# The last stage of a three-part kernel: out-weight conversion at the end of each block, plain products between the Strassen products, a branch moved earlier, and pools moved to other addresses

## The chip, the cores and the metric

The program runs on one core of a Trainium2 chip. The metric is the device time of one execution in microseconds (us); the median of several executions is compared. Five engines matter: PE (matrix products into PSUM banks), DVE and ACT (element work, both read PSUM), POOL (element work without PSUM) and SP (issues DMA). Each engine takes its own instructions strictly in the order in which they are written, and waits where an operand is not ready.

## What is computed

```python
a = x @ w_a            # x: 1536 x 512, from the two stages ahead (attention, a mixture of 8 experts)
b = x @ w_b            # w_a, w_b: 512 x 1536
out = (a * b) @ w_out  # w_out: 1536 x 512
```

The weights of this third part come in as 64-bit floats. The change is in this part, and at the end of the expert part, where it is prepared.

## The kernel before

Every float32 operand is split into a high part of a shorter format and a low remainder (`...h`, `...l`), and a product is three PE instructions: high by high, low by high, high by low. One such instruction streams 512 columns of its moving operand past 128 columns of weights that it loads first; the text calls it "a product".

The third part works on 12 blocks `f` of 128 columns of `w_a` and `w_b`, and on three row groups `c` of 512 tokens. Its token matrix has been put together by the experts in `y_dram`; row group 0 is `yT`, row groups 1 and 2 are loaded with `xload` into `XF` and split by `ysp`. Weights go through four steps per half block: `cload` (DMA issued by SP), `conv1` (two ACT instructions), `conv2` (three DVE instructions and one POOL add, L902), `conv3` (ACT cast of the high part, L913, and POOL subtraction for the low part, L914). The output weights `w_out` take the same steps; their halves are called `wo` and stand in `MW[12]` to `MW[17]`.

Blocks 0 and 1 are computed plainly: `first` (row group 0, 48 products), `plain(1, ..)` and `plain(2, ..)` (48 products each). For blocks 2 to 11 there is `seven(f)`. It computes row groups 0 and 1 with a Strassen scheme of seven half-size products on sums `S1` to `S4` of the tokens (made by `ssum` and `ysp`) and on sums of the weights (`tsum` on DVE, `tsplit` on ACT and POOL). The scheme takes 42 products on three banks `pa`, `pb`, `pc`. Its fifth product (`S3`) and its last (`A22`) both add into bank `pb`, and between them DVE reads the bank (L1292), so `A22` has to wait for that read. Row group 2 is computed plainly by `ab2` (24 products on `Y2`, "P2" in the title; P3, P5 and P7 are the Strassen products on `S3`, `S4` and the second half of `yT`); its result is multiplied on DVE (L1260) and split by `gate` (ACT L1186, DVE L1187).

After each odd block the two blocks' results meet the output weights: `both` puts 12 tiles in a list, and `fill(n)` takes n of them. `out_tile` is six products into one of three banks `o`, and one element instruction that adds the bank to the accumulator in `XF`. A pair of blocks has 6 tiles behind its odd block and 6 inside the next even one.

Between the experts and `seven` stands a branch (`tc.If`, L1067) that is not taken on these inputs. Whatever the branch might write counts as written by it: an instruction behind it that reads or overwrites such a tile waits until the writing engine has passed the branch, and an engine passes only when it has finished what it had before it. Ahead of the branch, DVE has the sums of the tokens (L1042) and `conv2` for the first output weights.

Tiles lie in pools that are stacked from the left (low addresses) or from the right end of SBUF. Before, the weights' pool `wA` starts at byte 20,000 of a partition, the pool `bg` (token accumulators, some expert weights, `S4`) at 52,768, the token sums and `Y2` at 85,536 to 134,688, the gate results `gh`, `gl` at 138,784 to 165,408, the pool `wM` (weights of block 0 and the output weights) at 176,096, and `yT` at 212,960.

Of the kernel before, what the change touches and what calls it, by code (L numbers as in the profile page):

```python
# [19 lines left out]
ALU = mybir.AluOpType  # L20
# [26 lines left out]
def moe_block_kernel(ctx, tc, qd, kd, vd, kt, vn, nv, wg, wg2, we, wm, out):  # L47
# [40 lines left out]

    wA = ctx.enter_context(tc.tile_pool(name="wA", bufs=4))
    bgp = ctx.enter_context(tc.tile_pool(name="bg", bufs=8, reuse_waits="tile"))  # L90

# [662 lines left out]

    def xload(c, g):
        if (c, g) not in XF:
            XF[c, g] = big("acc")[:, :].rearrange("p (k n) -> p k n", k=2)
        nc.sync.dma_start(XF[c, g], y_dram[2 * g:2 * g + 2, :, c * 512:(c + 1) * 512].rearrange("d p n -> p d n"))

# [164 lines left out]
    def ysplit(st, g, eng, yT):  # L924
# [15 lines left out]
        (6, 4): [(cload, nc.scalar)], (6, 8): [(cload, nc.scalar)],  # L940
        (7, 8): [(conv1, (1, 0))], (7, 9): [(conv2, (1, 0))], (7, 10): [(conv1, (1, 1))], (7, 11): [(conv2, (1, 1))],
        (7, 12): [(cload, nc.sync)], (7, 13): [(cload, nc.sync)], (7, 14): [(cload, nc.sync)],
    }
    for k, n in enumerate(CAPS):
        X = XT.pop(k)
        Hm = htiles(epp, n)
        nxt = tiles(CAPS[k + 1]) if k < NE - 1 else []
        gs = []

        def W(c):  # L950
            return EW[k, c]

        def tick(i):
            if k == 0 and i == 0:
                COL.extend(regs(range(7), [ACT], NTOK, "counts of tokens before an expert, or all tokens"))
                COL.extend(regs([7], [SP], NTOK, "counts of tokens before an expert, or all tokens"))
            if k == 1 and i == 0:
                rare.append(nc.values_load(ctl_i[0:1, 16:17], min_val=0, max_val=1, skip_runtime_bounds_check_because="a flag"))
            if k == 0 and i == 1:
                r_base()  # L960
                rt.append(r_token(ps, "h", 6, sc, i128, i96[:, 0:NT], tokid))
            if k < 2 and i % 4 == 2:
                next(rt[0], None)
            if k == 1 and i == 14:
                rsc.close()
                yp, pools["V"], pools["M"] = (
                    ctx.enter_context(tc.tile_pool(name=n_, bufs=1, side="right", reuse_waits="tile")) for n_ in ("yp", "cv", "wM"))
# [24 lines left out]
        for f in range(8):  # L992
            up(W, f, X, n, Hm, epp)
            if f == 2 and yq:
                yq.pop(0)()
            tick(f)
        for d in range(4):
            yq.append(down(W, d, Hm, n, COL[k], epp, bg=lambda h, d=d: tick(8 + 2 * d + h), q=nc.scalar if nxt else nc.sync))
            if d:
                yq.pop(0)()  # L1000
# [12 lines left out]

    def first():
        for (f, s_), pt in N0.items():
            mul(pt, wab(f, s_), yT, True)

    yq.pop(0)()
    for h in range(2):
        conv3((1, h))  # L1020
# [20 lines left out]
    def ssum(o, a, b, op):  # L1041
        V.tensor_tensor(o, a, b, op)  # L1042

    def sums():
        ssum(XF[1, 1], XF[1, 0], XF[1, 1], ALU.add)
        ssum(XF[1, 0], XF[0, 0], XF[1, 0], ALU.subtract)
        ssum(XF[0, 0], XF[1, 1], XF[0, 0], ALU.subtract)
        ssum(XF[0, 1], XF[0, 1], XF[0, 0], ALU.subtract)

    def c12(*js):  # L1050
        for j in js:
            conv1(j)
        conv2(*js)
        for _ in js:
            cload(nc.sync)

    for g in range(2):
        xload(2, g)
    ysp(XF[1, 0], S4, V)
    ysp(XF[1, 1], A22, V)  # L1060
    for h, l in (Y2, S2, S1, S3):
        A.copy(h[:, 0, 0:2], ident[:, 0:2])
        V.tensor_copy(l[:, 0, 0:2], ident[:, 0:2])
    sums()
    c12((12, 0), (12, 1))

    with tc.If(rare[0] == 1):  # L1067
        with ExitStack() as ls:
# [75 lines left out]
            lqs.close()  # L1144
            for c in (1, 0, 2):
                for g in range(2):
                    xload(c, g)
            for g in range(2):
                ysp(XF[0, g], [y[:, 2 * g:2 * g + 2] for y in yT], V)
            ysp(XF[1, 0], S4, V)  # L1150
            ysp(XF[1, 1], A22, V)
            sums()
            first()

# [33 lines left out]

    def evict(c, f, pp, h1=(), h2=()):

        a = tmp("a")
        A.copy(a, pp[0])
        run_all(h1)
        V.tensor_tensor(pp[1], a, pp[1], ALU.mult)
        low = gate(c, f, pp[1])
        run_all(h2)
        low()

    def plain(c, f, tags, h1=(), h2=()):

        pp = [t_ if not isinstance(t_, str) else bank(t_, {"ab": 2, "o": 3}.get(t_, 1)) for t_ in tags]
        for s_, pt in enumerate(pp):
# [3 lines left out]
            else:  # L1206
                mul(pt, wab(f, s_), Y2, True)
        evict(c, f, pp, h1, h2)

    def run_all(fs):  # L1210
        for f_, *x in fs:
            f_(*x)

    outs, items = [], []

    def out_tile(p, c, t_):
        po = bank("o", 3)
        for i, f in enumerate((2 * p, 2 * p + 1)):
# [4 lines left out]
            T.matmul(po, gl, wh, start=False, stop=(i == 1))  # L1223
        m, at = 4 * c + t_, XF[c, t_ // 2][:, t_ % 2]
        if p == 0:
            (A.copy if t_ % 2 else V.tensor_copy)(at, po)
        else:
            V.tensor_tensor(at, po, at, ALU.add)  # L1228
# [8 lines left out]
    def fill(n):  # L1237
        for _ in range(n):
            if items:
                out_tile(*items.pop(0))  # L1240

    def seven(f):

# [5 lines left out]
        nxt = [(f + 2, 0), (f + 2, 1)] if f < 10 else []  # L1249
        nxt += [WO[f + 1]] if f + 1 in WO else []  # L1250
        a = tmp("a")
# [10 lines left out]

        def side():
            if jobs:
                tsum(f + 1)
                tsplit(f + 1)
                conv2(*wo)
                for j in jobs + wo:
                    conv3(j)
                for _ in nxt:  # L1270
                    cload(nc.sync)

# [21 lines left out]
        V.tensor_tensor(u2, pc, u2, ALU.add)  # L1294
# [7 lines left out]
        low[1]()  # L1302
        for j in nxt:
            conv1(j)
# [8 lines left out]
    def both(p):  # L1313
        items.extend((p, c, t_) for c in (2, 0, 1) for t_ in range(4))
    evict(0, 0, (N0[0, 0], N0[0, 1]), (), [(conv3, (12, 0))])
    evict(0, 1, (N0[1, 0], N0[1, 1]), (), [(conv3, (12, 1))])
    pse.close()
    ps2 = ctx.enter_context(tc.tile_pool(name="ps2", bufs=1, space=PSUM, reuse_waits="tile"))
    pab = [bank("ab", 2) for _ in range(2)]
    for g in range(2):  # L1320
        ysp(XF[2, g], [y[:, 2 * g:2 * g + 2] for y in Y2], V)
    c12((2, 0), (2, 1))
    plain(1, 0, ("o", "pc"), (), [(tsum, 2), (conv3, (2, 0)), (conv3, (2, 1))])
    plain(1, 1, ("pa", "pb"), (), [(tsplit, 2), (ysp, XF[0, 0], S2, V)])
    plain(2, 0, pab, [(ysp, XF[1, 1], S1, V)], [(ysp, XF[0, 1], S4, V)])
    plain(2, 1, ("o", "pc"), [(ysp, XF[1, 0], S3, V)])
    c12((13, 0))
    for j in ((3, 0), (3, 1), (13, 1)):
        conv1(j)
    both(0)  # L1330
    fill(6)
    conv3((13, 0))
    for f in range(2, 12):
# [46 lines left out]
```

## Time and profile before

| | us |
|---|---|
| median of 3 runs | 629.22 (628.03 to 629.35) |
| the profiled execution, time | 632.77 |
| the profiled execution, span of its instructions | 631.1 |
| PE busy in the span | 575.5 (91%) |
| DVE, ACT, POOL busy | 419.8, 307.0, 246.9 |

The span runs from the first to the last profiled instruction. The third part begins at 299.5 us of the span. Busy time counts a waiting product not at all, and a product at a lower clock as longer.

### The profile page before, as it was taken

What the parts mean: (1) busy time and instruction counts of PE and PEld (TensorE: products, weight loads), DVE (VectorE), ACT (ScalarE), POOL (GpSimd) and SP (SyncE); (2) the same over time, 40 slices, a digit from 0 to 9 for tenths busy, and PEclk for the clock granted to TensorE, in tenths of its full rate; (3) what the DMA queues carried; (4) which work ended last, traced back from release to release, by engine and by line L of the source; (5) the groups of instructions that cost most, each with busy time, mean ns of one, the idle gap of its engine ahead of it and who ended that gap; (6) DMA issues with size and microseconds to landing.
All of it is one profiled execution on the core that took longest, in us unless ns stands there. A gap on an engine that the chain in (4) does not pass through costs nothing. (4 is left out here: it accounts for less than half of the span.)

```text
span 631.1 us, 9995 instructions
## 1 busy us (share of the span) xinstructions
PE 575.5 (91%) x3395; PEld 488.9 (77%) x3395; DVE 419.8 (67%) x988; ACT 307.0 (49%) x685; POOL 246.9 (39%) x227
## 2 busy tenths in 40 slices
PE   6998995799999999999894999899899899989994
PEld 4776774699999988999683788688688688778873
DVE  6878786686546868768766455576666576567462
ACT  5776881465566677765365434314405224331210
POOL 3000641544444645454342353334414614414224
PEclk9999997699999999999998899899899999979998
DMA  8477474467757798776530021111220302210013
GB/s 289 136 214 263 142 214 169 148 205 258 216 181 255 225 320 244 245 251 203 180 115 18 34 100 66 34 66 55 80 68 33 101 27 75 66 33 1 1 57 143
DMA packets 38656, 87.24 MB, mean 138 GB/s; under 512 B 5920, under 2 KB 16416, under 8 KB 38592
## 3 DMA queue, kind: packets, MB, share of 16 engines
q1 hardware_dynamic: 31680, 73.55, 35.7%
q10 hardware_dynamic: 4752, 6.00, 3.0%
q0 software_dynamic: 2160, 6.91, 3.0%
q8 instruction: 31, 0.51, 0.3%
q14 instruction: 33, 0.27, 0.1%
HBM read 73.25 MB, written 13.20 MB: 137 GB/s over the span
## 5 line engine op out<-in xcount | busy, mean ns | idle before, releaser
L117 POOL TENSOR_TENSOR wl<-st,wh 128x512 fp32r<-128x512 f32 x54 | 69.8, 1312 | 88.6 <-ACT wh L112 81.8
L902 POOL TENSOR_TENSOR tx<-tx,st 128x512 int32<-128x512 int32 x36 | 51.5, 1444 | 115.4 <-ACT p L1274 54.2
L112 ACT CAST wh<-st 128x1024 fp32r<-128x1024 f32 x64 | 67.3, 1054 | 31.1 <-DMA st<-we 30.5
L117 DVE TENSOR_TENSOR wl<-st,wh 128x1024 fp32r<-128x1024 f32 x37 | 53.3, 1442 | 29.0 <-ACT wh L112 28.7
L727 PE MATMUL ps_h<-x,wl 128*128 128x256 f32 (+5 forms) x256 | 69.8, 272 | 0.0
L727 PE MATMUL ps_y<-h,wl 128*128 128x256 f32 (+5 forms) x256 | 68.6, 268 | 0.0
L1221 PE MATMUL ps_o<-wh,gh 128*128 128x512 f32 x144 | 60.2, 418 | 7.0 <-ACT gh L1186 6.2
L1228 DVE TENSOR_TENSOR acc<-ps_o,acc 128x512 f32<-128x512 f32 x60 | 40.9, 690 | 34.0 <-PE ps_o L1223 31.8
L1223 PE MATMUL ps_o<-wh,gl 128*128 128x512 f32 x144 | 59.4, 412 | 1.9 <-DVE gl L1187 1.9
L1222 PE MATMUL ps_o<-wl,gh 128*128 128x512 f32 x144 | 59.9, 416 | 0.0
L523 ACT ACTIVATE pe<-pe,mx 128x256 f32<-128x256 f32 (+1 forms) x96 | 45.9, 480 | 22.4 <-DVE mx L519 22.4
L914 POOL TENSOR_TENSOR wl<-tx,wh 128x512 fp32r<-128x512 f32 x36 | 47.3, 1336 | 19.6 <-ACT wh L913 9.4
L723 PE MATMUL ps_y<-h,wh 128*128 128x448 f32 (+3 forms) x160 | 50.1, 372 | 2.8 <-DVE h L741 2.8
L727 PEld LDWEIGHTS ps_h<-x,wl 128*128 128x128 f32 x256 | 49.9, 195 | 0.0
L727 PEld LDWEIGHTS ps_y<-h,wl 128*128 128x128 f32 x256 | 48.5, 189 | 0.0
L1175 POOL TENSOR_TENSOR wl<-tt,wh 128x512 fp32r<-128x512 f32 x20 | 28.4, 1441 | 51.0 <-ACT wh L1173 51.0
L723 PE MATMUL ps_h<-x,wh 128*128 128x448 f32 (+3 forms) x160 | 48.2, 366 | 0.0
L1221 PEld LDWEIGHTS ps_o<-wh,gh 128*128 128x128 f32 x144 | 28.8, 200 | 15.5 <-ACT gh L1186 7.2
L519 DVE CUSTOM_DVE_ANT_0 pe<-ps_s,bias 128x256 f32<-128x256 f32 (+1 forms) x96 | 32.8, 398 | 8.2 <-PE ps_s L513 7.3
L1223 PEld LDWEIGHTS ps_o<-wh,gl 128*128 128x128 f32 x144 | 28.9, 201 | 9.9 <-DVE gl L1187 2.7
L913 ACT CAST wh<-tx 128x512 fp32r<-128x512 f32 x36 | 21.3, 619 | 28.5 <-POOL tx L902 28.5
L1222 PEld LDWEIGHTS ps_o<-wl,gh 128*128 128x128 f32 x144 | 28.9, 201 | 7.0
(317 smaller groups left out, 1526.6 us busy)
## 6 DMA issues: line engine op xcount, KB each, us to landing
st<-we SPq DMA_DIRECT2D x63, 512.0 KB, 4.7
st<-wm SPq DMA_DIRECT2D x32, 512.0 KB, 3.5
vc<-vd SPq DMA_DIRECT2D x16, 352.0 KB, 3.9
k<-kd SPq DMA_DIRECT2D x7, 464.0 KB, 7.0
y_dram<-zero SPq DMA_DIRECT2D x12, 256.0 KB, 6.5
x_dram<-x SPq DMA_DIRECT2D x6, 512.0 KB, 4.7
acc<-y_dram SPq DMA_DIRECT2D x6, 512.0 KB, 5.9
q<-qd SPq DMA_DIRECT2D x7, 384.0 KB, 5.9
```

Of the source, the lines that this page charges most:

```text
L112: A.copy(wh, st)
L117: eng.tensor_tensor(wl[:, r], st[:, r], wh[:, r].bitcast(F32), ALU.subtract)
L519: V.tensor_tensor_reduce(out=pe[:, t_, j, 0:n], in0=ps[:, j, t_, 0:n], in1=bias[2 * p + j][:, b0:b0 + n], op0=ALU.add, op1=ALU.min, scale= ...
L523: A.activation(pe[:, t_, j, 0:n], pe[:, t_, j, 0:n], AF.Exp, bias=mx[:, t_, j:j + 1], scale=-1.0, accum_out=sm[:, t_, j:j + 1])
L723: T.matmul(pt[:, 0:2 * n].rearrange("p (s n) -> p s n", s=2), a, M[:, k], start=(k == 0), stop=False)
L727: T.matmul(pt[:, 0:n], b, M[:, k, 0], start=False, stop=(k == last))
L902: lambda t=txi, l=l: G.tensor_tensor(t, t, l, ALU.add)))
L914: G.tensor_tensor(wl_, tx, wh.bitcast(F32), ALU.subtract)
L1221: T.matmul(po, gh, wh, start=(i == 0), stop=False)
L1222: T.matmul(po, gh, wl, start=False, stop=False)
L1223: T.matmul(po, gl, wh, start=False, stop=(i == 1))
L1228: V.tensor_tensor(at, po, at, ALU.add)
```

## The change

1. **Order inside `seven`.** `conv2` and the load of the output weights move from the middle of a block to its end (`rest`), and their `conv3` goes to the next block, behind the `conv3` of the block weights (`late`). In odd blocks `ab2(1)` and its split stand ahead of every `conv3`. The six products `A12` into bank `pa` move from ahead of `ab2(1)` to between `S3` and `S4`.
2. **Start of the third part.** The branch stands behind 24 of the 48 products of `first`; the other 24, the loads of row group 2, the token sums and `conv2` of the first output weights come behind it, interleaved with the plain products. Eight output tiles (before: six) run ahead of `seven(2)`; the first 12 tiles' copies are all on ACT, in another order of row groups. `conv3` of block 1 and `conv1` of the first output weights go into the last expert; one load moves into the expert before it.
3. **Places.** `wA` and `bg` are stacked from the right. Now the token sums and `Y2` lie at 20,000 to 69,152, `gh`, `gl` at 75,296 to 99,872, `wM` at 110,560, `yT` at 126,944, `bg` at 163,808 and `wA` at 196,576.

```diff
-    wA = ctx.enter_context(tc.tile_pool(name="wA", bufs=4))
-    bgp = ctx.enter_context(tc.tile_pool(name="bg", bufs=8, reuse_waits="tile"))
+    wA = ctx.enter_context(tc.tile_pool(name="wA", bufs=4, side="right"))
+    bgp = ctx.enter_context(tc.tile_pool(name="bg", bufs=8, side="right", reuse_waits="tile"))
...
-        (7, 12): [(cload, nc.sync)], (7, 13): [(cload, nc.sync)], (7, 14): [(cload, nc.sync)],
+        (6, 14): [(cload, nc.sync)], (7, 12): [(cload, nc.sync)],
+        (7, 13): [(conv3, (1, 0)), (conv1, (12, 0))], (7, 15): [(conv3, (1, 1)), (conv1, (12, 1))],
...
-    first()
+    first(0)
...
-    ysp(XF[1, 0], S4, V)
-    ysp(XF[1, 1], A22, V)
...
-    sums()
-    c12((12, 0), (12, 1))
 
     with tc.If(rare[0] == 1):
...
-        def side():
-            if jobs:
-                tsum(f + 1)
-                tsplit(f + 1)
-                conv2(*wo)
-                for j in jobs + wo:
-                    conv3(j)
-                for _ in nxt:
-                    cload(nc.sync)
+        def rest():
+            for j in wo:
+                c2(j)
+                late.append((conv3, j))
+            for j in nxt:
+                conv1(j)
...
             fill(4)
-        side()
-        mul(pa, wab(f, 0, 2, 4), A12, False, True, True)
+        if jobs:
+            tsum(f + 1)
+            tsplit(f + 1)
         if f % 2:
             ab2(1)
             low[2]()
-        else:
+        for j in jobs:
+            conv3(j)
+        while late:
+            f_, j = late.pop(0)
+            f_(j)
+        for j in wo:
+            conv1(j)
+        for _ in nxt:
+            cload(nc.sync)
+        if f % 2 == 0:
             fill(2)
         mul(pb, T3, S3, False, True, True)
         V.tensor_tensor(v, pb, v, ALU.add)
+        mul(pa, wab(f, 0, 2, 4), A12, False, True, True)
         mul(pc, wab(f, 1, 2, 4), S4, False, True, True)
...
         if f % 2:
             both(f // 2)
-            fill(6 if f < 11 else 12)
+            fill(3)
+            rest()
+            fill(3 if f < 11 else 9)
         else:
             ab2(0)
+            rest()
             ab2(1)
             low[2]()
...
+    for g in range(2):
+        xload(2, g)
+    first(1)
+    c2((12, 0), (12, 1))
+    e = [evict(0, f, (N0[f, 0], N0[f, 1])) for f in range(2)]
+    ysp(XF[1, 0], S4, V)
...
+    both(0, (0, 1, 2))
+    e[1]()
+    ysp(XF[0, 0], S2, V)
+    fill(2)
+    ssum(XF[0, 1], XF[0, 1], XF[0, 0], ALU.subtract)
+    conv3((2, 0))
+    fill(1)
+    ysp(XF[0, 1], S4, V)
+    conv3((2, 1))
+    fill(1)
```

ACT in an odd block (`seven(5)`), from the copy of the first Strassen product to the split of `ab2`'s result, before:

```order
L1258 COPY a<-ps_ab 128x512
L1173 CAST wh<-tt 128x1024
L913 CAST wh<-tx 128x512 x3
L1186 CAST gh<-ps_ab 128x512
L1186 CAST gh<-ps_pa 128x512
```

and in the changed kernel, the same place (its lines are numbered anew):

```order
L1237 COPY a<-ps_ab 128x512
L1146 CAST wh<-tt 128x1024
L1159 CAST gh<-ps_ab 128x512
L913 CAST wh<-tx 128x512 x3
L885 ACTIVATE tx<-st_6823 128x512
L887 ACTIVATE st_6823<-st_6823 128x512
L1159 CAST gh<-ps_pa 128x512
```

The cast `gh<-ps_ab` has moved ahead of the three `conv3` casts, and a `conv1` pair stands where none was.

POOL in the same block, before: two adds of the block weights, the two low halves of the weight sums, the add of the output weights and three low parts.

```order
L902 TENSOR_TENSOR tx<-tx,st_6794 128x512
L902 TENSOR_TENSOR tx<-tx,st_6796 128x512
L1175 TENSOR_TENSOR wl<-tt,wh 128x512 x2
L902 TENSOR_TENSOR tx<-tx,st_6798 128x512
L914 TENSOR_TENSOR wl<-tx,wh 128x512 x3
```

and in the changed kernel:

```order
L902 TENSOR_TENSOR tx<-tx,st_6748 128x512
L902 TENSOR_TENSOR tx<-tx,st_6750 128x512
L1148 TENSOR_TENSOR wl<-tt,wh 128x512 x2
L914 TENSOR_TENSOR wl<-tx,wh 128x512 x3
L902 TENSOR_TENSOR tx<-tx,st_6823 128x512
```

The add of the output weights now follows the three low parts, the last of which belongs to the output weights that were added one block earlier.

DVE ahead of the branch, from the last expert results on, before:

```order
L749 TENSOR_TENSOR yt<-ps_y,yt 128x176 x3
L1039 TENSOR_TENSOR S4l<-acc,S4h 128x1024
L1039 TENSOR_TENSOR A22l<-acc,A22h 128x1024
L1063 CAST Y2l<-ident 128x2
L1063 CAST S2l<-ident 128x2
L1063 CAST S1l<-ident 128x2
L1063 CAST S3l<-ident 128x2
L1042 TENSOR_TENSOR acc<-acc 128x1024 x4
L897 TENSOR_SCALAR tx<-tx 128x512 x2
L899 TENSOR_SCALAR tx<-tx 128x512 x2
L900 SCALAR_TENSOR_TENSOR tx<-st_5267,tx 128x512
L900 SCALAR_TENSOR_TENSOR tx<-st_5277,tx 128x512
```

and in the changed kernel:

```order
L749 TENSOR_TENSOR yt<-ps_y,yt 128x176
L897 TENSOR_SCALAR tx<-tx 128x512
L899 TENSOR_SCALAR tx<-tx 128x512
L900 SCALAR_TENSOR_TENSOR tx<-st_4969,tx 128x512
L749 TENSOR_TENSOR yt<-ps_y,yt 128x176 x3
L1043 COMPARE_AND_BRANCH
```

Between the last expert result and the branch nothing is left on DVE; the splits, the sums and `conv2` stand behind it.

## Rows read from the trace of the kernel before

**Rows 1.** Windows, third part: us, busy (instructions) of PE, PEld, DVE, ACT, POOL; clock.

```profile
299.50:357.87 58.37, 47.47 (x183) 36.59 (x182) 38.04 (x56) 29.28 (x50) 18.41 (x13) 0.88 0.30 95
357.87:622.30 264.43, 251.99 (x1057) 202.97 (x1055) 161.57 (x284) 81.90 (x139) 106.08 (x83) 0.97 0.17 57
```

**Rows 2.** Waits of PE, third part: line, released by, total us, times, longest.

```profile
PE ps_pb L1007 <- DVE v L1292: 12.4, 4, 3.1
PE ps_o L1221 <- ACT gh L1186: 6.2, 2, 4.7
```

**Rows 3.** The chain that ended last, inside `seven(5)`: start us, us, step.

```profile
446.44 1.25 POOL tx L902
447.72 0.62 ACT wh L913
448.33 0.49 ACT gh L1186
448.85 0.69 DVE gl L1187
449.54 0.61 DVE v L1292
450.20 0.50 PE ps_pb L1007
```

**Rows 4.** Timeline of PE in `seven(4)` and `seven(5)`: start us, us, instruction.

```profile
413.86 0.39 PE L1221 MATMUL ps_o<-wh,gh 128*128 128x512 f32 x1
...
419.46 0.39 PE L1007 MATMUL ps_pa<-yTh,wh 128*128 128x512 f32 x1
...
427.76 0.39 PE L1007 MATMUL ps_ab<-Y2h,wh 128*128 128x512 f32 x1
...
433.20 0.39 PE L1007 MATMUL ps_pa<-yTh,wh 128*128 128x512 f32 x1
...
434.60 0.39 PE L1007 MATMUL ps_pb<-S2h,wh 128*128 128x512 f32 x1
...
451.41 0.63 PE L1008 MATMUL ps_pb<-A22l,wh 128*128 128x512 f32 x1
451.84 0.63 PE L1009 MATMUL ps_pb<-A22h,wl 128*128 128x512 f32 x1
```

**Rows 5.** Timelines of DVE, POOL and ACT around the branch; brackets: idle before, releaser.

```profile
305.57 4.99 DVE L1042 TENSOR_TENSOR acc<-acc 128x1024 f32<-128x1024 f32 x4
312.63 2.88 POOL L902 TENSOR_TENSOR tx<-tx,st 128x512 int32<-128x512 int32 x2 [9.48 <-DVE tx L900]
315.60 0.58 ACT L1192 COPY a<-ps_n 128x512 f32<-128x512 f32 x1 [10.00 <-POOLq L1067]
```

**Rows 6.** Timelines of POOL in `seven(4)` and `seven(5)`, and of ACT in `seven(5)`.

```profile
422.98 2.78 POOL L1175 TENSOR_TENSOR wl<-tt,wh 128x512 fp32r<-128x512 f32 x2 [7.38 <-ACT wh L1173]
...
438.02 2.90 POOL L902 TENSOR_TENSOR tx<-tx,st 128x512 int32<-128x512 int32 x2 [7.24 <-issue]
443.68 2.76 POOL L1175 TENSOR_TENSOR wl<-tt,wh 128x512 fp32r<-128x512 f32 x2 [2.75 <-ACT wh L1173]
447.64 3.74 POOL L914 TENSOR_TENSOR wl<-tx,wh 128x512 fp32r<-128x512 f32 x3
442.55 1.05 ACT L1173 CAST wh<-tt 128x1024 fp32r<-128x1024 f32 x1 [1.65 <-DVE tt L1168]
```

**Rows 7.** Timelines of POOL and DVE just ahead of the branch.

```profile
300.60 2.55 POOL L914 TENSOR_TENSOR wl<-tx,wh 128x512 fp32r<-128x512 f32 x2 [2.33 <-ACT wh L913]
302.08 2.15 DVE L1039 TENSOR_TENSOR S4l<-acc,S4h 128x1024 fp32r<-128x1024 f32 x1 [1.70 <-ACT S4h L1037]
304.15 1.21 DVE L1039 TENSOR_TENSOR A22l<-acc,A22h 128x1024 fp32r<-128x1024 f32 x1
```

**Rows 8.** Timeline of PE in `first`, weights in `wM`: start us, us, instruction.

```profile
303.19 0.39 PE L1008 MATMUL ps_n<-yTl,wh 128*128 128x512 f32 x1
...
304.55 0.39 PE L1008 MATMUL ps_n<-yTl,wh 128*128 128x512 f32 x1
```

More of the change, by code (lines that the diff above doesn't have):

```diff
@@ L940, in moe_block_kernel @@
         (6, 4): [(cload, nc.scalar)], (6, 8): [(cload, nc.scalar)],
-        (7, 8): [(conv1, (1, 0))], (7, 9): [(conv2, (1, 0))], (7, 10): [(conv1, (1, 1))], (7, 11): [(conv2, (1, 1))],
-        (7, 12): [(cload, nc.sync)], (7, 13): [(cload, nc.sync)], (7, 14): [(cload, nc.sync)],
+        (7, 8): [(conv1, (1, 0))], (7, 9): [(conv2, (1, 0))], (7, 10): [(conv1, (1, 1)), (cload, nc.sync)], (7, 11): [(conv2, (1, 1))],
+        (6, 14): [(cload, nc.sync)], (7, 12): [(cload, nc.sync)],
+        (7, 13): [(conv3, (1, 0)), (conv1, (12, 0))], (7, 15): [(conv3, (1, 1)), (conv1, (12, 1))],
     }
@@ L955, in tick @@
                 COL.extend(regs(range(7), [ACT], NTOK, "counts of tokens before an expert, or all tokens"))
-                COL.extend(regs([7], [SP], NTOK, "counts of tokens before an expert, or all tokens"))
+                COL.extend(regs([7], [SP, ACT], NTOK, "counts of tokens before an expert, or all tokens"))
             if k == 1 and i == 0:
@@ L965, in tick @@
                 rsc.close()
-                yp, pools["V"], pools["M"] = (
-                    ctx.enter_context(tc.tile_pool(name=n_, bufs=1, side="right", reuse_waits="tile")) for n_ in ("yp", "cv", "wM"))
+                pools["V"], yp, pools["M"] = (
+                    ctx.enter_context(tc.tile_pool(name=n_, bufs=1, side="right", reuse_waits="tile")) for n_ in ("cv", "yp", "wM"))
                 yT.extend(yp.tile([P, 4, 512], F32R, name=n_) for n_ in ("yTh", "yTl"))
@@ L997, in moe_block_kernel @@
         for d in range(4):
-            yq.append(down(W, d, Hm, n, COL[k], epp, bg=lambda h, d=d: tick(8 + 2 * d + h), q=nc.scalar if nxt else nc.sync))
+            yq.append(down(W, d, Hm, n, COL[k], epp, bg=lambda h, d=d: tick(8 + 2 * d + h), q=nc.scalar if nxt or d == 3 else nc.sync))
             if d:
@@ L1012, in wab, with first @@
         return [w[:, :].rearrange("p (s k n) -> p s k n", s=2, k=4)[:, s_, k0:k1] for w in MW[f]]
-    def first():
-        for (f, s_), pt in N0.items():
-            mul(pt, wab(f, s_), yT, True)
+    def first(f):
+        for s_ in range(2):
+            mul(N0[f, s_], wab(f, s_), yT, True)
     yq.pop(0)()
-    for h in range(2):
-        conv3((1, h))
     N0 = {(f, s_): ps.tile([P, 512], F32, tag="h", bufs=6, name="ps_n") for f in range(2) for s_ in range(2)}
-    first()
+    first(0)
     ep.close()
@@ L1042, in ssum @@
         V.tensor_tensor(o, a, b, op)
[L1044 to L1054, printed above, removed]
-            cload(nc.sync)
-    for g in range(2):
-        xload(2, g)
-    ysp(XF[1, 0], S4, V)
-    ysp(XF[1, 1], A22, V)
-    for h, l in (Y2, S2, S1, S3):
-        A.copy(h[:, 0, 0:2], ident[:, 0:2])
-        V.tensor_copy(l[:, 0, 0:2], ident[:, 0:2])
-    sums()
-    c12((12, 0), (12, 1))
     with tc.If(rare[0] == 1):
@@ L1144, in moe_block_kernel @@
             lqs.close()
-            for c in (1, 0, 2):
+            for c in (1, 0):
                 for g in range(2):
-                    xload(c, g)
+                    xload(c, g, nc.scalar)
             for g in range(2):
                 ysp(XF[0, g], [y[:, 2 * g:2 * g + 2] for y in yT], V)
[L1150 to L1153, printed above, removed]
+            first(0)
     m2 = ctx.enter_context(tc.tile_pool(name="m2", bufs=1, side="left", reuse_waits="tile"))
@@ L1187, in gate, with evict, first_, second @@
         return lambda: V.tensor_tensor(gl, a, gh[:, :].bitcast(F32), ALU.subtract)
-    def evict(c, f, pp, h1=(), h2=()):
+    def evict(c, f, pp):
         a = tmp("a")
[L1192 to L1199, printed above, removed]
+        def first_():
+            A.copy(a, pp[0])
+            V.tensor_tensor(pp[1], a, pp[1], ALU.mult)
+        def second():
+            gate(c, f, pp[1])()
+        return first_, second
+    def plain(c, f, tags):
         pp = [t_ if not isinstance(t_, str) else bank(t_, {"ab": 2, "o": 3}.get(t_, 1)) for t_ in tags]
@@ L1207, in plain @@
                 mul(pt, wab(f, s_), Y2, True)
[L1208 to L1212, printed above, removed]
+        return pp
     outs, items = [], []
@@ L1223, in out_tile @@
             T.matmul(po, gl, wh, start=False, stop=(i == 1))
-        m, at = 4 * c + t_, XF[c, t_ // 2][:, t_ % 2]
+        m, at = 4 * c + t_, XF[(c + 2) % 3, t_ // 2][:, t_ % 2]
         if p == 0:
-            (A.copy if t_ % 2 else V.tensor_copy)(at, po)
+            A.copy(at, po)
         else:
@@ L1240, in fill, with c2 @@
                 out_tile(*items.pop(0))
+    late = []
+    def c2(*js):
+        conv2(*js)
+        for _ in js:
+            cload(nc.sync)
     def seven(f):
@@ L1249, in seven @@
         nxt = [(f + 2, 0), (f + 2, 1)] if f < 10 else []
-        nxt += [WO[f + 1]] if f + 1 in WO else []
         a = tmp("a")
@@ L1288, in seven @@
             low[2]()
-        else:
+        for j in jobs:
[6 more added lines that the diff above has]
+        for _ in nxt:
+            cload(nc.sync)
+        if f % 2 == 0:
             fill(2)
@@ L1302, in seven, with both, ev @@
         low[1]()
-        for j in nxt:
-            conv1(j)
         if f % 2:
             both(f // 2)
-            fill(6 if f < 11 else 12)
+            fill(3)
+            rest()
+            fill(3 if f < 11 else 9)
         else:
             ab2(0)
+            rest()
             ab2(1)
             low[2]()
[L1313 to L1316, printed above, removed]
+    def both(p, order=(2, 0, 1)):
+        items.extend((p, c, t_) for c in order for t_ in range(4))
+    def ev(c, f, pp):
+        for f_ in evict(c, f, pp):
+            f_()
+    for g in range(2):
[4 more added lines that the diff above has]
+    ysp(XF[1, 0], S4, V)
+    e[0][0]()
+    e[0][1]()
+    ysp(XF[1, 1], A22, V)
+    conv1((2, 0))
+    ev(0, 1, (N0[1, 0], N0[1, 1]))
     pse.close()
@@ L1319, in moe_block_kernel @@
     pab = [bank("ab", 2) for _ in range(2)]
+    p10, p11 = plain(1, 0, ("o", "pc")), plain(1, 1, ("pa", "pb"))
+    for h in range(2):
+        conv3((12, h))
     for g in range(2):
         ysp(XF[2, g], [y[:, 2 * g:2 * g + 2] for y in Y2], V)
[L1322 to L1332, printed above, removed]
+    conv1((2, 1))
+    ssum(XF[1, 1], XF[1, 0], XF[1, 1], ALU.add)
+    ev(1, 0, p10)
+    c2((2, 0), (2, 1))
+    ev(1, 1, p11)
+    p20, p21 = plain(2, 0, pab), plain(2, 1, ("o", "pc"))
+    ev(2, 0, p20)
+    tsum(2)
+    tsplit(2)
+    conv1((13, 0))
+    ssum(XF[1, 0], XF[0, 0], XF[1, 0], ALU.subtract)
+    e = evict(2, 1, p21)
+    e[0]()
+    ssum(XF[0, 0], XF[1, 1], XF[0, 0], ALU.subtract)
+    both(0, (0, 1, 2))
[8 more added lines that the diff above has]
+    fill(1)
+    ysp(XF[1, 1], S1, V)
+    fill(1)
+    conv1((3, 0))
+    fill(1)
+    ysp(XF[1, 0], S3, V)
+    conv1((3, 1))
+    fill(2)
+    c2((13, 0))
+    late.append((conv3, (13, 0)))
     for f in range(2, 12):
```

5 lines of the change are left out of this document (2 added, 3 removed).

## The prediction

> **What bounds the kernel now.** I read the windows of the third part first. PE is busy in 252.0 of the 264.4 us from 357.87 on, and in 47.5 of the 58.4 us before that, at granted clocks of 0.97 and 0.88 [rows 1]; DVE comes next with 161.6 and 38.0 us. So PE is the bound, and what can be gained is the time in which it waits or runs at the lower of its two levels (1.2 instead of 2.4 GHz). To see how much that is, I work out what the same products cost without either, from the starts of products in the timeline: 24 of row group 2 begin within 433.20 - 427.76 = 5.44 us, that is 0.2267 us each, and 24 of output tiles within 419.46 - 413.86 = 5.60 us, 0.2333 each [rows 4].
>
> The window from 357.87 on (call it B) holds ten blocks of 66 products and 66 tiles of six. Of the 660, 540 go at 0.2267 (122.4 us), and 120 on `yT` at the tiles' 0.2333 (28.0 us; six of them take 434.60 - 433.20 = 1.40 us [rows 4]); the 396 of the tiles take 92.4 us. Sum 242.8 us. The window is 264.4, so 21.6 us are lost. The waits of PE name 12.4 of them: bank `pb` waits four times for DVE's L1292, up to 3.1 us [rows 2]. The other 9.2 us I put down to the lower level: products that follow such a wait run at it, two of them starting 451.84 - 451.41 = 0.43 us apart [rows 4], and a mean clock of 0.97 is 6% of 264 us at half speed, which costs about 8 us [rows 1].
>
> Why `pb` waits shows the chain of `seven(5)`: the POOL add of the output weights, L902, ends at 447.7; ACT's third `conv3` needs it; behind that cast stands, in ACT's order, the cast `gh` of row group 2; then `gl` on DVE, and behind `gl` the read of `pb`, which ends at 450.15, after which A22 starts [rows 3]. The row group that is cast there has nothing to do with the add. It only stands behind it.
>
> The first window (A, 58.4 us) holds 144 plain products at 0.2267 (32.6 us) and 36 of the first six tiles at 0.2333 (8.4 us): 41.0. The other 17.4 are lost. Two waits in the third part for ACT's L1186 make 6.2 us [rows 2], and the branch is behind the rest: DVE still has 4.99 us of sums from 305.57 on, `conv2` after that, POOL's adds until 315.5, and ACT, which has stood idle for 10.0 us, passes the branch only then and can copy the first result at 315.60 [rows 5].
>
> **The blocks after the change.** In an odd block ACT's `gh` now stands ahead of `conv3`. With the times of `seven(5)`: the adds of the block weights end at 440.9; the sums on DVE took from there until 442.5, and ACT's split 1.05, until 443.6 [rows 6]. The row group's banks are full 1.4 us earlier than before, since six products `A12` that stood ahead of them move behind; DVE's multiplication no longer waits for `conv2`. `gh`, `gl` and the read of `pb` follow at 0.6, 0.7 and 0.6 [rows 3], so the read ends by about 445.6. A block begins with 18 Strassen products, then in odd blocks the 24 of row group 2, then S3, A12, S4 and A22. From the block's start at 433.20 [rows 4], 48 products at 0.2267 and 12 at 0.2333 stand ahead of A22: it comes up at 433.2 + 10.9 + 2.8 = 446.9, which leaves 1.3 us to spare. So the four waits go, 12.4 us, and with them the reason for the 9.2.
>
> What is late next: the output weights' low part. It is the third L914 behind the split. The low halves of the sums end at 443.68 + 2.76 = 446.4, three low parts take 3.74 [rows 6], so it ends at 450.2. It is the half for the odd block `f`, which a tile reads first in its fifth product; the other half was made a block earlier. The fifth product of the first tile behind A22 comes up at 446.9 + 1.36 (six products of A22) + 0.93 (four of the tile) = 449.2. That is 1.0 us late at worst, nothing at best (the casts on ACT may run a little ahead). I take 0.6, four times: +2.4 us.
>
> Even blocks: in `seven(4)` the low halves end at 422.98 + 2.78 = 425.8; two low parts at 1.25 put the next block's weights at 428.3 [rows 6]. The next block starts 23.4 us after this one began, near 433.2 [rows 4], so 4.9 us are spare. `conv2`, `conv1` and the loads that move to the end only have to be done before the next block's sums. I take 0. POOL's 106 us and ACT's 82 in B [rows 1] leave room.
>
> B also loses two tiles, which run ahead: 12 products, 2.8 us. B: 242.8 - 2.8 = 240.0, which is 24.4 less.
>
> **The start after the change.** Nothing but the last expert results stands on DVE ahead of the branch, and POOL's low parts, done at 300.60 + 2.55 = 303.2 in the old order [rows 7], are earlier now. PE reaches the branch after 24 products, at 299.5 + 5.4 = 304.9. SP has the last expert's results to write ahead of it, which no row here times. I let all have passed by about 306; I take 1.0 for PE's own step over it and for what PE loses if SP is last. Then PE has 24 more products, 5.4 us, and needs the splits of row group 1 by 311.5: `conv2` and the low part of `S4`, 2.15 us at most [rows 7], are done by 310. The tiles that follow wait for copies on ACT that stand behind splits; by walking ACT's and DVE's order with durations of before I find about 1.5 us. A after: 32.6 + 48 tile products x 0.2333 = 11.2, + 2.5 = 46.3 us; 12.1 less. DVE's 38.0 us would fill 82% of it, so it is the part where cover is thinnest.
>
> **The places.** Products differ by what they read: `yT` moving goes at 0.2267 with weights in `wM`, six products in 304.55 - 303.19 = 1.36 us [rows 8], and at 0.2333 with weights in `wA`; row group 2 with weights in `wA` goes at 0.2267, tiles at 0.2333 [rows 4]. So the place of the moving operand alone does not set the pitch. The bounds: gained 0.0067 on the 120 and on the tiles' 432, 3.7 us; lost 0.0067 on the 540, 3.6 us, and 3% on the 276 us that PE is busy outside these windows, 8.1, together 11.7. I take 0, as pairs of places change and I see no side for either.
>
> The Trainium skill, page "SBUF — State Buffer", section "Who interferes with whom", gives PE read ports of its own, shared with no engine. By that the place would cost nothing at all; the rows' two pitches at one clock say that something about the operands matters, by 3%.
>
> **Sum.** A -12.1, B -24.4, output weights +2.4, and +1.5 (from 0 to 3) for what dense DVE and POOL work beside each other costs, the next paragraph's mechanism taken at a small part: -32.6. The profiled execution took 632.8, so 600.2; it lies 3.55 above the median of 629.22, so the median becomes 596.6, say **597**.
>
> **Rivals.** *DVE and POOL hinder each other (608).* The low part of `S4` took 2.15 us while POOL made low parts, and the same form took 1.21 just after, when POOL was idle [rows 7]: 0.94 us more. At the start DVE's work is now packed into 46 instead of 58 us, beside 13 POOL instructions [rows 1]. If each costs DVE that, its 38.0 us become 50, and with the 5 us before it gets its rows A is 55: 9 to 11 of the 12 us are gone. Against it: many of DVE's forms there read a PSUM bank and only one SBUF operand. The Trainium skill, in the section named above, states the rule: a VectorE operation with two SBUF operands and a GpSimd operation lock each other out. The trace agrees in this one pair of rows.
>
> *The low part stalls and drops the clock (610).* If each of the four is late by the full 1.0 and the clock falls as after the old waits, 9.2 / 4 = 2.3 each, it is 3.3 x 4 = 13.2 instead of 2.4.
>
> *The next block's weights are late (over 629).* This ends on the other side. If the chain of an even block, sums, split, low parts, comes more than 4.9 us later than now, the five odd blocks start late. At 2.3 us for the clock each, all 33 us are eaten when 5 x (late - 4.9 + 2.3) = 33, that is at 9.2 us late. It needs ACT's `conv1` or the loads to be late by a third of a block, where ACT's work of before fills 31% of B. Little speaks for it.
>
> *The places cost it all (slower).* They would have to add 33 us: on the 1,236 products of the third part (1,056 + 180) that is 27 ns each, four times the 6.7 that any two kinds differ by. I count it with the last.
>
> **How the numbers follow.** The likeliest case, 588 to 603 (places gained 3.7, extra terms nothing, at the low end; lateness 1.0 and places 3.6 lost at the high one), gets 0.70. The two that give back a third or so, 603 to 615, together get 0.22, small gains above that 0.02, no change 0.01, slower 0.05. The range 589 to 610 leaves out the lowest corner and the upper half of the second case. Within 0.2% (1.3 us, about what a measurement can tell from nothing): 0.01; faster 0.94; slower 0.05.
>
> **What the profile will show.** Right: L1292 no longer releases PE; the granted clock from `seven(2)` on is near 1.0; the time from the first plain product to `seven(2)` is about 46 us; ACT copies its first result before 312; the wait behind A22, if any, is on POOL's L914, under 1.1 us, four times. Wrong: a DVE that is busy nearly all the time between 306 and 346 with passes near 2 us beside POOL's; a wait at the first product of odd blocks on `wl`; pitches above 0.2333 in the blocks, or shorter ones for tiles, which would say that places matter.

## The result, and the profile after

| | before | changed |
|---|---|---|
| median of 4 runs, us | 629.29 (628.03 to 629.73) | 597.34 (596.67 to 598.00) |
| profiled execution: time, span | 632.77, 631.1 | 596.95, 595.2 |
| PE busy in the span | 575.5 (91%) | 562.1 (94%) |

The ratio is 0.9495, 95% interval 0.9477 to 0.9514. The forecast was 597. That the median agrees to 0.4 us says little by itself, since terms can cancel; so the stretches come first. Windows of the changed kernel: start of the third part, blocks, and what follows the last product (start and end; then us; busy time and instructions of PE, PEld, its weight loads, DVE, ACT and POOL; granted clock; DMA share; GB/s):

```profile
299.68:346.17 46.49, 44.99 (x195) 35.86 (x193) 30.86 (x41) 26.29 (x45) 17.61 (x12) 1.00 0.26 87
346.17:589.18 243.01, 242.43 (x1045) 195.67 (x1043) 165.91 (x290) 86.70 (x146) 106.69 (x85) 1.00 0.18 64
589.18:595.20 6.02, 0.17 (x1) 0.00 (x0) 0.69 (x1) 0.00 (x0) 1.91 (x2) 0.84 0.35 132
```

The same for before, with its blocks cut behind the last product:

```profile
299.50:357.87 58.37, 47.47 (x183) 36.59 (x182) 38.04 (x56) 29.28 (x50) 18.41 (x13) 0.88 0.30 95
357.87:622.47 264.60, 252.16 (x1057) 202.97 (x1055) 161.63 (x285) 81.90 (x139) 106.25 (x83) 0.97 0.17 57
622.47:631.10 8.63, 0.16 (x1) 0.00 (x0) 1.32 (x2) 0.00 (x0) 2.37 (x3) 0.65 0.24 92
```

The start takes 11.9 us less, the blocks 21.6, the tail 2.6, and the granted clock is 1.00 in both stretches where it was 0.88 and 0.97. The tail's part is no part of the change: in the profiled execution of before, DVE stood idle for 2.18 us ahead of its last add, on something that the profile only calls remote. In every other profile of this document, those of two kernels with the old start among them (order_only, gate_first below), the stretch behind the last product takes 6.0 to 6.2 us. So 2.6 of the 3.55 us by which that execution lies above its median are this tail.

```profile
625.28 0.69 DVE L1228 TENSOR_TENSOR acc<-ps_o,acc 128x512 f32<-128x512 f32 x1 [2.18 <-remote]
```

What PE waits for in the third part now, against [rows 2] (line, released by, total us, times, longest):

```profile
PE ps_o L1009 <- DVE A22l L1038: 0.6, 1, 0.6
PE ps_n L1008 <- DVE tx L897: 0.5, 1, 0.5
PE ps_o L1193 <- ACT acc L1198: 0.3, 1, 0.3
```

The read of `pb` (L1292 before, L1278 now) is gone from it. For the weight loads (PEld) of the same part the same view has one more:

```profile
PEld ps_o L1194 <- POOL wl L914: 2.3, 4, 0.6
```

That is the predicted new edge, four times. `seven(5)` in the timelines of ACT, DVE, POOL and PE, against [rows 3, 6]:

```profile
423.40 1.05 ACT L1146 CAST wh<-tt 128x1024 fp32r<-128x1024 f32 x1 [1.16 <-DVE tt L1141]
425.14 0.59 ACT L1159 CAST gh<-ps_ab 128x512 fp32r<-128x512 f32 x1 [0.69 <-DVE ps_ab L1239]
425.62 1.66 ACT L913 CAST wh<-tx 128x512 fp32r<-128x512 f32 x3
...
425.76 0.69 DVE L1160 TENSOR_TENSOR gl<-ps_ab,gh 128x512 fp32r<-128x512 f32 x1 [0.65 <-ACT gh L1159]
426.37 0.68 DVE L1278 TENSOR_TENSOR v<-ps_pb,v 128x512 f32<-128x512 f32 x1
...
427.05 3.82 POOL L914 TENSOR_TENSOR wl<-tx,wh 128x512 fp32r<-128x512 f32 x3
...
428.29 0.40 PE L1008 MATMUL ps_pb<-A22h,wh 128*128 128x512 f32 x1
```

The cast `gh` stands ahead of the three casts, the read of `pb` ends at 427.05, and A22 starts at 428.29: 1.24 us to spare, where 1.3 was forecast. The last of POOL's low parts ends at 430.87, later than a tile's fifth product would have begun.

### The profile page after: what moved, and what is told of

The parts are those of the page before. It is cut to its first block, busy times and chain, and to the rows that moved or that the text cites. A ratio compares the mean times of both kernels' runs of the same rounds, so it can differ in the third digit from the quotient of the medians.

```text
span 595.2 us, 9990 instructions
## 1 busy us (share of the span) xinstructions
PE 562.1 (94%) x3395; PEld 479.8 (81%) x3395; DVE 418.2 (70%) x978; ACT 309.4 (52%) x687; POOL 246.3 (41%) x227
## 5 line engine op out<-in xcount | busy, mean ns | idle before, releaser
L112 ACT CAST wh<-st 128x1024 fp32r<-128x1024 f32 x64 | 67.4, 1054 | 30.9 <-DMA st<-we 30.2
L117 DVE TENSOR_TENSOR wl<-st,wh 128x1024 fp32r<-128x1024 f32 x37 | 52.0, 1405 | 27.1 <-ACT wh L112 26.8
L914 POOL TENSOR_TENSOR wl<-tx,wh 128x512 fp32r<-128x512 f32 x36 | 48.7, 1377 | 23.8 <-ACT wh L913 23.8
L1194 PE MATMUL ps_o<-wl,gh 128*128 128x512 f32 x144 | 57.3, 398 | 0.6
L1193 PE MATMUL ps_o<-wh,gh 128*128 128x512 f32 x144 | 56.9, 395 | 0.3 <-ACT acc L1198 0.3
L1195 PE MATMUL ps_o<-wh,gl 128*128 128x512 f32 x144 | 56.9, 395 | 0.0
L1148 POOL TENSOR_TENSOR wl<-tt,wh 128x512 fp32r<-128x512 f32 x20 | 25.7, 1307 | 48.2 <-ACT wh L1146 48.2
L1146 ACT CAST wh<-tt 128x1024 fp32r<-128x1024 f32 x10 | 10.5, 1049 | 47.5 <-DVE tt L1141 47.5
L1008 PE MATMUL ps_ab<-Y2h,wh 128*128 128x512 f32 x88 | 34.7, 395 | 0.0
L1010 PE MATMUL ps_ab<-Y2h,wl 128*128 128x512 f32 x88 | 34.5, 392 | 0.0
L1009 PE MATMUL ps_ab<-Y2l,wh 128*128 128x512 f32 x88 | 34.2, 388 | 0.0
```

Of the source, the lines that this page charges most:

```text
L112: A.copy(wh, st)
L117: eng.tensor_tensor(wl[:, r], st[:, r], wh[:, r].bitcast(F32), ALU.subtract)
L914: G.tensor_tensor(wl_, tx, wh.bitcast(F32), ALU.subtract)
L1008: T.matmul(pt, wh[:, k, :], yh[:, k, :], start=start and k == 0, stop=False, skip_group_check=more)
L1193: T.matmul(po, gh, wh, start=(i == 0), stop=False)
L1194: T.matmul(po, gh, wl, start=False, stop=False)
```

## The experiments

All medians below stand beside runs of before on the same chip: 630.24 in the first group, 629.01 in the second, 628.67 in the third. A difference between two changed kernels under about 2 us in the median can't be told apart; there I compare stretches of the profiles.

**Order alone** (order_only: start, branch and places as before). The new `seven` with `late` and `c2`, as the diff of the change shows them, is put into the kernel before; one `conv1` leaves the start.

```diff
...
-    for j in ((3, 0), (3, 1), (13, 1)):
+    for j in ((3, 0), (3, 1)):
```

> The kernel before with the new order inside seven alone (start, branch and places as before). My theory: the four waits for L1292 (12.4 us) and the lower clock behind them (9.2) go, the output weights' low part costs about 1.7, the start stays at 58 us: 609 to 611 us. Rival (the start or the places made most of the gain): above 620.

Measured: 610.49, ratio 0.9681 (0.9652 to 0.9709), which is 20 us. Among its waits of PE there is none of bank `pb` for DVE's `v` any more, only the start's and the short new ones:

```profile
PE ps_o L1221 <- ACT gh L1186: 6.4, 2, 4.8
...
PE ps_o L1222 <- POOL wl L914: 1.2, 4, 0.5
```

The blocks take 245.60 us at a clock of 1.00 (357.47 to 603.07), where before took 264.60. The rival falls: most of the gain is the order's.

**The old order with the new start and places** (old_order). `seven` of before in the changed kernel; what it expects to have been done ahead (`conv1` and `conv3` of (13, 1) and (13, 0)) is put back at the end of the start.

```diff
...
     c2((13, 0))
-    late.append((conv3, (13, 0)))
+    conv1((13, 1))
+    conv3((13, 0))
```

> The changed kernel with the order inside seven of before; the new start and the new places stay. My theory: only the start's 11.9 us are gained, the four waits for DVE's read of pb are there again: 616 to 619 us. If the start's gain were given back by the blocks, or the order needed it: 625 or more.

Measured: 621.54, ratio 0.9875 (0.9846 to 0.9905): 8.7 us gained, 2.5 us past the upper end expected. The start did take 46.75 us; the blocks gave some back.

```profile
PE ps_pb L1008 <- DVE v L1264: 13.7, 5, 3.9
PE ps_o L1193 <- ACT acc L1198: 2.8, 2, 2.5
```

There is a fifth wait for the read of `pb`, 0.9 us, in `seven(2)`, the longest is 3.9 instead of 3.1, and a tile waits 2.5 us for ACT's copy. That last one comes from the start of this run, not from the old order: the `conv1` that was put back there waits for its load, and the copies stand behind it on ACT.

```profile
354.05 0.66 ACT L885 ACTIVATE tx<-st 128x512 f32<-128x512 f32 x1 [5.34 <-DMA st<-wm]
...
356.14 1.57 ACT L1198 COPY acc<-ps_o 128x512 f32<-128x512 f32 x3
```

Without it the start alone would have given some 11 us, an estimate (8.7 and 2.5). So 20 and 11 come near the 32 measured.

**Only the row group's gate ahead** (gate_first). In before, the row group's products and gate go, in odd blocks, ahead of the output weights' `conv2` and of every `conv3`; these and the loads are split off `side` as `side2`. Nothing else moves.

```diff
         side()
+        if f % 2 == 0:
+            side2()
         mul(pa, wab(f, 0, 2, 4), A12, False, True, True)
         if f % 2:
             ab2(1)
             low[2]()
+            side2()
```

> The kernel before with one thing moved: in odd blocks ab2(1) and its gate stand ahead of the output weights' conv2 and of every conv3; A12 and the start stay. My theory: the row group's cast no longer waits for the add, but DVE's conv2 for the output weights (1.4 us) now stands ahead of the read of pb, and A22 is only 12 products behind: a wait of about 1.4 us is left of 3.1, 615 to 622 us. If the cast's place in ACT's order had nothing to do with the wait: 629. If it is all that the order inside seven brings: 610.

Measured: 617.51, ratio 0.9792 (0.9762 to 0.9821).

```profile
PE ps_pb L1007 <- DVE v L1298: 6.4, 4, 1.6
```

The four waits are halved, 12.4 to 6.4, from one move; from 340 us on 13 products run at the lower level instead of 46 (those whose next one starts 0.40 to 0.45 us later), none of them behind these four waits. That it was the cast's place on ACT, and not the place of DVE's multiplication ahead of `conv2`, shows in before's `seven(5)`: there DVE had multiplied by 445.17 and then stood idle for 3.68 us until `gh` came. The other half of the wait is DVE's `conv2`, which in this run stands between `gl` and the read of `pb` (444.27 to 445.79 in `seven(5)`). The full order takes it away and puts A12 ahead of A22; no run has one of the two alone.

**Places undone** (old_places), in the changed kernel: `wA`, `bg` left, `yT`'s pool ahead of the staging pool.

```diff
-    wA = ctx.enter_context(tc.tile_pool(name="wA", bufs=4, side="right"))
-    bgp = ctx.enter_context(tc.tile_pool(name="bg", bufs=8, side="right", reuse_waits="tile"))
+    wA = ctx.enter_context(tc.tile_pool(name="wA", bufs=4))
+    bgp = ctx.enter_context(tc.tile_pool(name="bg", bufs=8, reuse_waits="tile"))
...
```

> The changed kernel with the pools wA and bg stacked from the left again and yT's pool ahead of the staging pool, as before. My theory: places are worth nothing net, as the products' pitches only change sides (products on the sums 0.2289 to 0.2322 now, 0.2267 to 0.230 before; yT 0.2314 now, 0.2333 before): 596 to 598 us. Rival (low addresses of the moving operands made part of the gain): 600 or more.

Measured: 596.41, ratio 0.9461 (0.9434 to 0.9487), an interval that overlaps the changed kernel's. The low addresses brought nothing that a median shows.

**The output weights' `conv3` first** (late_first) in odd blocks:

```diff
-        for j in jobs:
-            conv3(j)
-        while late:
-            f_, j = late.pop(0)
-            f_(j)
+        js = [j for _, j in late]
+        late.clear()
+        for j in js + jobs if f % 2 else jobs + js:
+            conv3(j)
```

> The changed kernel, in odd blocks with conv3 of the output weights ahead of conv3 of the two block halves. My theory: the output weights' low part is made 2.5 us earlier, which ends the four waits of the tile's fifth product (1.65 us in the changed kernel); the block halves come 1.3 us later and have over 6 us to spare: 595 to 596.5 us. Rival (the wait only moves to the next block's first product): 597 to 599.

Measured: 594.56, ratio 0.9463 (0.9437 to 0.9489), 0.4 us below the range expected. Its blocks (the window's columns as above):

```profile
345.02:586.35 241.33, 241.33 (x1045) 195.60 (x1043) 165.92 (x290) 86.71 (x146) 106.68 (x85) 1.00 0.18 65
```

243.01 - 241.33 = 1.68 us less, the 1.65 that the four waits cost. PE does not stand idle in its blocks at all, and no wait appears at the next block.

**Late POOL, 4 us** (pool_late3), and **8 us** (pool_late6). In even blocks the first low half of the weight sums is computed 4 times (below) or 7 times; the values stay the same.

```diff
-        for a in (0, 512):
+        for a in (0, 512) if f % 2 == 0 else (0,) * 4 + (512,):
```

> The changed kernel with the first low half of the weight sums computed four times instead of once in even blocks (three more POOL instructions of 1.3 us; the same values are written again). The block's low parts end 5.3 us ahead of the next block's start in the changed kernel, so 4 us of lateness cost nothing: 597 to 598. If POOL and DVE hinder each other (0.94 us for each POOL instruction), DVE gets up to 14 us more work, but has room: up to 600. If the spare time were misread: 602 or more.

Measured: 600.97, ratio 0.9562 (0.9530 to 0.9594): 3.6 us more than the changed kernel, not nothing. The next block's first product doesn't wait. The tile behind A22 of that next block does:

```profile
PE ps_o L1194 <- POOL wl L914: 4.6, 4, 2.0
```

The way there, in DVE's timeline of `seven(4)`, while POOL makes its (now later) low parts:

```profile
413.10 0.48 DVE L897 TENSOR_SCALAR tx<-tx 128x512 f32<-128x512 f32 x1
413.62 1.41 DVE L899 TENSOR_SCALAR tx<-tx 128x512 int32<-128x512 int32 x1
415.06 1.67 DVE L900 SCALAR_TENSOR_TENSOR tx<-st,tx 128x512 int32<-128x512 int32 x1
```

The same three passes in the changed kernel, with POOL idle:

```profile
411.96 0.42 DVE L897 TENSOR_SCALAR tx<-tx 128x512 f32<-128x512 f32 x1
412.41 0.43 DVE L899 TENSOR_SCALAR tx<-tx 128x512 int32<-128x512 int32 x1
412.87 0.69 DVE L900 SCALAR_TENSOR_TENSOR tx<-st,tx 128x512 int32<-128x512 int32 x1
```

Two passes take 0.98 us longer each. DVE had 1.2 us of idle time behind them, which takes up most of it; the next `conv2`, POOL's adds, the sums and the low parts of the odd block still come 0.75 us later in the block, and the chain with the least room, the output weights' low part, hits PE: from the starts of products, 2.1 us once and 1.0 three times, where it was 0.3.

> The same with six more POOL instructions, 7.9 to 8.3 us, in each of the five even blocks. The spare 5.3 us are used up: each next block starts 2.6 to 3.0 us late, 13 to 15 us in all, and up to 2.3 us for the lower clock behind each wait: 611 to 624 us. If the rival of late weights starts elsewhere (or not at all): 598.

Measured: 616.74, ratio 0.9803 (0.9770 to 0.9837), 19.4 us more.

```profile
PE ps_pa L1010 <- POOL wl L914: 11.5, 5, 3.7
```

Five odd blocks now start late, at the third product, by 2.1 us from the starts of products (the first by 3.9). From 340 us on 41 products run at the lower level, 0.2 us more each, 8.2 us. 11.5 + 8.2 = 19.7 makes up the difference.

**Where the branch stands.** All 48 products of `first` ahead of it (ahead48, below), or none (ahead0, both calls behind the branch):

```diff
     first(0)
+    first(1)
...
```

> The changed kernel with all 48 products of first ahead of the branch. In the changed kernel DVE and ACT stand idle for 3 us and pass the branch at 305.4, just after PE's 24th product (304.96) and also just when the last expert rows are written. Theory A (they wait for PE's arrival): they pass at about 310.5, the splits of row group 1 come 5 us later, PE waits for them: 600 to 605 us. Theory B (they wait for the rows' write): they pass at 305.4 as now: 596 to 598.5.

Measured: 598.76, ratio 0.9543 (0.9515 to 0.9571), just past theory B's upper end (598.5). In this profile the third part begins at 297.34; DVE passes at 302.80, 5.5 us after that, as in the changed kernel (305.42 after 299.68: 5.7). In brackets, `DVEq` is DVE's own sequencer, which takes the branch.

```profile
302.80 0.76 DVE L897 TENSOR_SCALAR tx<-tx 128x512 f32<-128x512 f32 x2 [2.79 <-DVEq L1044]
```

DVE does not wait for PE's arrival. ACT, though, copies its first result only once PE has passed the branch (at 309.72), and PE waits three times:

```profile
309.99 0.47 PE L1008 MATMUL ps_o<-S4h,wh 128*128 128x512 f32 x1 [1.55 <-PEq L1044]
312.65 0.50 PE L1008 MATMUL ps_o<-A22h,wh 128*128 128x512 f32 x1 [1.06 <-ACT A22h L1037]
313.91 0.50 PE L1009 MATMUL ps_o<-A22l,wh 128*128 128x512 f32 x1 [0.76 <-DVE A22l L1039]
```

The start takes 48.95 us (297.34 to 346.29) instead of 46.49.

> The changed kernel with all 48 products of first behind the branch. Theory A (engines wait for each other there): PE waits from 299.7 until DVE and ACT arrive at about 302.5, the splits are then ready in time: 598 to 600 us. Theory B (the last expert rows' write has to land): PE waits until about 305, 5.3 us, of which 0.7 for the step over the branch and 0.6 for the later split come back: 601 to 604.

Measured: 603.28, ratio 0.9596 (0.9580 to 0.9612).

```profile
305.79 0.79 PE L1008 MATMUL ps_n<-yTh,wh 128*128 128x512 f32 x1 [5.57 <-ACTq L1042]
```

PE stands 5.6 us at the branch and eight of its next products run at the lower level. In time both runs are about as theory B has them: the branch opens about 3 us after DVE's last expert result. Theory B's reason does not hold for DVE, though. In the changed kernel ACT issues the last row write at 302.38 (the change moved it there from SP), and in the trace it lands 2.4 us later, ahead of DVE's first pass at 305.42. In pool_late6 it lands 3.5 us after its issue, at 304.1, and DVE has passed 0.6 us earlier:

```profile
300.57 0.34 ACTq L750 DMA_DIRECT2D y_dram<-yt  x1
...
303.44 0.76 DVE L897 TENSOR_SCALAR tx<-tx 128x512 f32<-128x512 f32 x2 [2.91 <-DVEq L1043]
...
304.44 0.96 SPq L758 DMA_DIRECT2D acc<-y_dram  x2
```

Only SP, whose next load reads the rows, keeps its distance to the landing: 0.36 us in all ten kernels with the new start. DVE's first pass comes 2.8 to 3.4 us after its last expert result in all ten. What fills this step stays open. Four packets of the instruction queues run in it, in the changed kernel as in pool_late6, so the loading of the code behind the branch is a rival; no run tried it.

**Operands at the same place within 128 bytes** (late_first_pad64): a pad of 64 bytes at the right end, on top of the kernel with the output weights first.

```diff
+    padp = ctx.enter_context(tc.tile_pool(name="pad", bufs=1, side="right"))
+    padp.tile([P, 16], F32, name="pad")
```

> The same with a pad of 64 bytes at the right end of SBUF, so that weights and moving operands of left and right pools stand at the same place within 128 bytes. In the traces of both kernels a product whose two operands stand at the same place takes 0.2267 to 0.2275 us, and one with them 64 bytes apart 0.229 to 0.2333. My theory: that relation sets the pitch, so tiles, yT and the products on the sums all go at about 0.227: 2.8 + 0.6 + 1.6 = 5 us less than the kernel without the pad, 590 to 592 us. Rival (left or right half of SBUF, or the pool's other traffic, sets it): no change from the kernel without it.

Measured: 595.25, ratio 0.9472 (0.9444 to 0.9501), and in the profile 242.40 us for the blocks, 1.1 us more than without the pad. My theory falls: tiles stay at 0.2330, the products of row group 2 become slower (0.2289 to 0.2333), and those on `S4`, whose two operands moved together, become faster (0.2288 to 0.2267). The pitch does depend on where operands lie, but not on their relation within 128 bytes.

**The best of both** (late_first_old_places): output weights first, old places.

> The kernel with the output weights' conv3 first, and with the pools at their old places. My theory: places are worth under 1 us: 593.5 to 595.5, and in the trace the blocks take about 0.8 us less than late_first's 241.1 us. Rival (low addresses help): 596 or more.

Measured: 593.62, ratio 0.9447 (0.9430 to 0.9465). Its blocks:

```profile
346.14:586.64 240.50, 240.50 (x1045) 195.45 (x1043) 165.55 (x290) 86.67 (x146) 106.66 (x85) 1.00 0.18 65
```

0.83 us less than with the new places, as expected, too little for the medians to show (594.56 and 593.62, with overlapping intervals). It is the fastest kernel here; the profile shows 2.5 us of that in the blocks against the changed kernel, 1.7 for the waits and 0.8 for the pitches.

## Why the prediction was right

**Blocks.** Predicted: 240.0 for the products, 2.4 for the output weights and part of a 1.5 that was common to blocks and start, so 242.4 to 243.9. Measured 243.01. The four waits and the lower clock behind them went, as the chain had it; the new order alone shows 20 us, and the row group's gate moved ahead alone takes away half of the waits. The output weights' low part was the next edge: the price was 0.41 us each (a wait of 0.31 and a first product 0.1 longer), 1.65 in all, where 0.6 and 2.4 stood. Putting that conversion first takes away exactly this.

**Start.** Predicted 46.3, measured 46.49. The branch opened at 305.4 ("about 306"), PE lost 0.7 us at it (1.0 taken), 0.8 at A22's split, and about 0.6 at a copy (1.5 taken for copies). The prediction left open what opens the branch. It is not PE's arrival (ahead48); DVE's own work was done 3 us earlier; and for DVE it is not the landing of the rows either (pool_late6). The time of the opening was an allowance that came out right, and its cause stays open. What the place of the branch gains is 24 products of cover while the others stand still; with 48 the start is 2.5 us longer in the profile, with none some 6, PE's wait at the branch counted in. That the work of DVE behind the branch was the old obstacle agrees with [rows 5]; no run put only that work back.

**DVE and POOL beside each other** (1.5, rival 608). The mechanism is there and its size at one place is near what [rows 7] said. In the changed kernel's start, DVE's low part of `S4` and POOL's two adds run together and both are slower than elsewhere:

```profile
307.97 2.33 DVE L1038 TENSOR_TENSOR S4l<-acc,S4h 128x1024 fp32r<-128x1024 f32 x1
312.51 1.23 DVE L1038 TENSOR_TENSOR A22l<-acc,A22h 128x1024 fp32r<-128x1024 f32 x1 [0.26 <-ACT A22h L1036]
...
307.53 3.93 POOL L902 TENSOR_TENSOR tx<-tx,st 128x512 int32<-128x512 int32 x2 [5.49 <-DVE tx L900]
```

1.1 us each (two such adds take 2.80 at 418.98). This meeting reached PE: behind `S4l` DVE multiplies (310.22), ACT casts `gh` (310.94) and `A22h` (311.42), DVE makes `A22l` (312.51), and PE waits 0.8 us for it; 1.1 us earlier it would have been there in time. That is read from the timelines; no run takes the meeting away. A second one, at `Y2l`, made two passes 0.9 us longer (317.44, 3.35 us) and reached nothing. But the other POOL instructions of the estimate's 13 meet such a pass only in smaller overlaps, and DVE's busy time in the start even fell, 38.0 to 30.9, since work and copies left that stretch. So the rival was wrong by its count of meetings, not by their price. The Trainium skill, page "SBUF — State Buffer", section "Who interferes with whom", also lets VectorE's one-input `tensor_scalar` take the shared pair in some of its modes; pool_late3 agrees, with L899 at 1.41 instead of 0.43 us, beside POOL's subtractions; L897, also a `tensor_scalar`, took 0.48 instead of 0.42 there.

**Places** (0). Measured 0.8 us against the change in the blocks, no difference in the medians. Within the bounds, but the 0 had no reason beyond "no side for either"; what sets a pitch stays open. From the starts of 24 products: 0.2289 for row group 2 in the changed kernel, 0.2267 at the old places, tiles at 0.233 in both.

**Late weights** (the rival on the slower side). pool_late6 shows that it works as written: spare time of 5.3 us (4.9 forecast), then a wait per block and the lower clock behind it (8.2 / 5 = 1.6 us each, 2.3 taken), 19.4 us for 8 us of lateness. pool_late3 shows what the prediction missed: lateness inside the spare time of an even block is not free, because it reaches the odd block's shorter chain through DVE.

**Profile to median.** The sum gave 600.2 for the profiled execution and took 3.55 off for its distance to the median. The execution after took 596.95 and lies at its median. So the distance was that one execution's own, 2.6 us of it in the tail; taking it off was right.

**How much of the 0.4 us is luck.** The mechanism came out as written; that the sum did so closely is in part misses against each other. The products of the blocks take 241.3 us without any wait (late_first) where 240.0 stood: 0.8 are the places, and 0.5 is there at the old places too, since products on `S2` and `S4` start 0.230 us apart and those on `S3` 0.228, and not 0.2267 as the 540 were counted. Against this stand 0.75 too much for the output weights and the extra 1.5, of which only the 0.8 at `A22l` is seen, inside the start's 46.49. Two rivals were also priced too high by their own terms: 9 to 11 us given back, with the 1.5 taken off, makes 604 to 606 and not 608, and 13.2 instead of 2.4 makes 607 and not 610.

## What to carry to other kernels

An in-order engine passes on the wait of whatever stands ahead. Here a cast for another purpose, queued behind one late conversion, cost four waits of 3 us and two thirds as much again in clock, and the cure was to start the late item's conversion a block earlier and to write its last step behind the others. When such a chain is cut, look for the next one with the least room (here 0.4 us too late, four times) and see whether an item with 6 us of room stands in front of it. A step's spare time has to be measured to the nearest reader along every engine it shares, not to its own consumer alone.

## What the runs showed of the hardware

- A product's pitch (from one start to the next) at one granted clock (1.00) varied from 0.2267 to 0.2333 us with the addresses of its operands: row group 2 took 0.2267, 0.2289 and 0.2333 in three layouts of the same code. Which property of the addresses does it was not found; the place within 128 bytes does not explain it.
- The branch held DVE 2.8 to 3.4 us after its last work in all ten kernels with the new start, wherever PE stood, and in one of them DVE passed 0.6 us before the last write ahead of the branch had landed. What fills the time was not found.
- A wait of PE had no fixed price in clock: after 2.7 us from the starts of products (2.5 in the list of waits) in old_order the products went on at 0.23 us; in pool_late6 waits of 2.1 us by the same count were followed, a few products on, by 7 or 8 at 0.427 us.
